# The last projection of a one-token attention kernel: wo in four loads, loop steps of eight, four column groups, one stored row

## The chip, the core and the metric

The kernel runs on one core of one Trainium2 chip. The time is the device's time of one execution in microseconds (us), of which medians are given. The profile shows one execution more closely. It calls TensorE "PE" (its weight loads "PEld"), VectorE "DVE", ScalarE "ACT", GpSimd "POOL", and SyncE's queue of DMA issues "SPq". The profile's "span" runs from its first to its last instruction; the time of the same run is 2.0 to 2.5 us longer. The granted clock is the share of TensorE's full clock that the throttle let through.

## The reference, cut to what matters

One token x of 512 elements. Branch A is attention of one query per head over 32 heads and 16384 stored keys and values of 128 elements each. Branch B is a small gated mixer. A gate g mixes the two.

```python
q = (x @ wq).reshape(1, 1, 32, 128)                      # 32 heads
p = softmax(q @ k_cache.T * 128 ** -0.5)                 # 16384 keys per head
a = (p @ v_cache).reshape(1, 1, 4096) @ wo               # wo: 4096 x 512
b = mixer(x, w_in, w_sp, b_sp, w_out)                    # 1 x 1 x 512
return g * a + (1 - g) * b                               # 1 x 1 x 512, bf16
```

Keys and values are 256 MB (2 x 32 x 16384 x 128 x 2 bytes). wo is 4 MB, the last that is loaded and the last that is used: out = sum over k of o2[:, k].T @ wo_k, for 32 slices wo_k of 128 x 512, with o2 the attention's result of 128 x 32.

## The kernel before

Keys and values stream through three buffers of 8 MB. wo goes into one of these buffers behind the last values, so its load starts when the last keys have been used. What matters here is the end: the loads of wo, the loop over k, and the store.

```python
WG = 4                                          # slices per loop step
WO_CUTS = (0, 8, 16, 24, 26, 28, 30, 31, 32)    # eight loads of wo, in slices of k
WIDE = 24                                       # slices done in the loop
# ... cut ...
def pe_wide(e):
    # ... cut: registers, waits for o2 ...
    with e.Fori(0, WIDE // WG) as t:            # six steps
        # ... four matmuls, k = 4t .. 4t+3, one in each column group of 32 of the array,
        #     each 1 x 512 into its own partition of the bank d_ps
        registers_first(nc, n, lambda: take(e, wo_s))    # wait for the load of these slices
        ins.then_inc(pe.sem, 1)
        warm(e, 1)                              # one matmul of 128x512 on zeros, to keep PE busy
        # ... registers ...
w_ok = act.op(lambda e: e.copy(out=d_sb[:, :], in_=d_ps), wait=[(pe.sem, pe.n)], mark=True)
for j, (a, b) in enumerate(zip(WO_CUTS[:-1], WO_CUTS[1:])):
    for k in range(max(a, WIDE), b):            # k = 24 .. 31
        for s in range(2):                      # two column groups of 256 columns
            # ... matmul into a_ps[32 * s], waits for load j before its first k
    if b == 28:
        # ... add: ones.T @ d_sb (fp32) into a_ps, in two halves of 256; waits for w_ok
r0_ok = dve.op(...copy a_ps[0, 0:256] to res[0, :]...)
r1_ok = act.op(...copy a_ps[32, 0:256] to res[32, :]...)
sp.op(lambda e: e.dma_start(out=out.rearrange("a b (c m) -> (a b c) m", c=2),
                            in_=res[0:33:32, :]), wait=[r0_ok, r1_ok], inc=(st_out, 16))
```

"k" below is such a slice of wo; one k is 1 KB in each of 128 partitions.

The softmax here doesn't subtract the row's maximum and nothing guards it: scores larger than these inputs give would overflow.

## Time and profile before

| | |
|---|---|
| time, median of the first 6 runs | 654.58 us (653.52 to 656.73) |
| profiled execution | 653.67 us, span 651.6 us |
| load queue | 279.58 MB, 99.4% of 16 engines' span |
| PE, DVE busy | 62%, 52% of the span |

The page of the kernel before, its parts 1 and 3 (busy us, share of the span, instructions; then queue, packets, MB, share of the 16 DMA engines):

```profile
span 651.6 us, 7678 instructions
...
PE 405.9 (62%) x2354; PEld 46.7 (7%) x1326; DVE 338.8 (52%) x162; ACT 43.5 (7%) x112; POOL 2.1 (0%) x9
...
q1 hardware_dynamic: 6772, 279.58, 99.4%
```

The loads fill the span. Only what follows the last byte can be anything else. The timeline of the last microseconds of the kernel before (start, duration, engine, line, operation, output <- inputs, count, and in brackets the idle time before it and what ended that):

```profile
643.55 0.39 PE L99 MATMUL ps_all<-bufs,o 128*1 x4 [0.48 <-PEq L82]
643.87 0.39 PE L443 MATMUL ps_all<-zero,ident 128*128 128x512 bf16 x1
644.31 0.39 PE L99 MATMUL ps_all<-bufs,o 128*1 x4
...
647.36 0.39 PE L99 MATMUL ps_all<-bufs,o 128*1 x4
...
648.00 0.60 PE L669 MATMUL ps_all<-bufs,o 128*1 128x256 bf16 x8
648.44 0.60 PE L676 MATMUL ps_all<-d_sb,const-float32-1.0 128*1 128x256 f32 x4
648.87 0.61 PE L669 MATMUL ps_all<-bufs,o 128*1 128x256 bf16 x8
...
649.51 0.41 DVE L680 CAST res<-ps_all 1x256 bf16<-1x256 f32 x1 [6.55 <-PE ps_all L669]
649.97 0.61 SPq L684 DMA_DIRECT2D out_dram<-res  x1
```

L99 is the loop (four matmuls a step, 0.75 us apart), L443 the warming matmul, L669 the last eight k, L676 the add. From 643.55 on the view marks idle time of PE before the first line alone: PE is working off a backlog. The view of the chain that ended last (start, duration, what) says the same. As far back as it goes, from 645.06 to the last matmul, it is PE's work, and no load is in it:

```profile
645.11 0.39 PE ps_all L99 x4
...
649.04 0.45 PE ps_all L669 x8
```

The loads of wo, in the view of their line:

```profile
L602 SPq DMA_DIRECT2D bufs<-in_A_wo_dram x8: 328/432/7735, 619.1 to 629.6; - x8
...
DMA to landing us min/median/max: 19.3/26.4/26.9
```

The last is issued at 629.6 and lands 19.3 us later, at 648.9. The last matmul ends 0.54 us after that (649.47 in the trace's records).

### The profile page before, as it was taken

What the parts mean: (1) busy time and instruction counts of PE and PEld (TensorE: products, weight loads), DVE (VectorE), ACT (ScalarE), POOL (GpSimd) and SP (SyncE); (2) the same over time, 40 slices, a digit from 0 to 9 for tenths busy, and PEclk for the clock granted to TensorE, in tenths of its full rate; (3) what the DMA queues carried; (4) which work ended last, traced back from release to release, by engine and by line L of the source; (5) the groups of instructions that cost most, each with busy time, mean ns of one, the idle gap of its engine ahead of it and who ended that gap; (6) DMA issues with size and microseconds to landing.
All of it is one profiled execution on the core that took longest, in us unless ns stands there. A gap on an engine that the chain in (4) does not pass through costs nothing. (4 is left out here: it accounts for less than half of the span.)

```text
span 651.6 us, 7678 instructions
## 1 busy us (share of the span) xinstructions
PE 405.9 (62%) x2354; PEld 46.7 (7%) x1326; DVE 338.8 (52%) x162; ACT 43.5 (7%) x112; POOL 2.1 (0%) x9
## 2 busy tenths in 40 slices
PE   4466856747386564747756375575737657477776
PEld 0100010000101000010000101000010100001012
DVE  4687708356280745618265470835629074565600
ACT  2101010000001000010100001000000100001011
POOL 1000000000000000000000000000000000000000
PEclk9678797969779696987969798786979968698979
DMA  9999999999999999999999999999999999999997
GB/s 388 439 437 451 435 426 426 451 435 402 451 451 426 410 451 439 435 414 451 435 426 426 451 435 406 447 451 426 410 451 439 435 414 451 435 416 437 426 419 314
DMA packets 6781, 279.60 MB, mean 429 GB/s; under 512 B 760, under 2 KB 1020, under 8 KB 1532
## 3 DMA queue, kind: packets, MB, share of 16 engines
q1 hardware_dynamic: 6772, 279.58, 99.4%
q8 instruction: 1, 0.02, 0.0%
q10 hardware_dynamic: 8, 0.00, 0.0%
HBM read 279.58 MB, written 0.00 MB: 429 GB/s over the span
## 5 line engine op out<-in xcount | busy, mean ns | idle before, releaser
L538 DVE TENSOR_TENSOR bufs<-bufs,qb x64 | 281.4, 4418 | 171.1 <-DVEq L82 171.1
L86 PE MATMUL ps_all<-bufs,ident 128*128 x960 | 261.9, 427 | 0.0
L456 PE MATMUL ps_all<-bufs,ident 128*128 x64 | 28.6, 447 | 157.0 <-PEq L82 157.0
L99 PE MATMUL ps_all<-bufs,p_t 128*8 x1024 | 79.8, 391 | 53.3 <-PEq L82 53.2
L522 DVE TENSOR_REDUCE s_sb<-ps_all 128x64 f32<-128x512 f32 x64 | 44.0, 688 | 95.5 <-DVEq L82 95.5
L550 ACT ACTIVATE p_t<-s_sb 64x256 f32 (+1 forms) x32 | 13.3, 414 | 440.4 <-ACTq L82 440.0
L456 PEld LDWEIGHTS ps_all<-bufs,ident 128*128 128x128 bf16 x64 | 6.3, 99 | 371.2 <-issue 371.2
L99 PEld LDWEIGHTS ps_all<-bufs,p_t 128*8 x1024 | 17.2, 82 | 164.4 <-issue 164.4
L490 PE MATMUL ps_all<-pick,d_sb 128*128 128x2 f32 x128 | 16.9, 254 | 14.8 <-PEq L82 14.8
L490 PEld LDWEIGHTS ps_all<-pick,d_sb 128*128 128x128 f32 x128 | 15.7, 192 | 26.3 <-issue 26.3
L559 ACT COPY d_sb<-ps_all 128x512 f32<-128x512 f32 x16 | 9.4, 585 | 104.5 <-ACTq L82 104.5
L443 PE MATMUL ps_all<-zero,ident 128*128 128x512 bf16 x25 | 9.7, 389 | 0.0
L86 PE MATMUL ps_all<-zero,ident 128*128 128x512 bf16 x32 | 9.5, 379 | 0.0
L564 ACT CAST ps_all<-zero 128x512 f32<-128x512 bf16 x15 | 8.8, 589 | 1.7
L360 PE MATMUL ps_all<-stats,const-float32-1.0 128*128 128x2 f32 x2 | 0.6, 362 | 9.2 <-DVE stats L358 9.2
L628 DVE RECIPROCAL rl<-ps_all 128x32 f32<-128x32 f32 x1 | 0.4, 358 | 11.3 <-PE ps_all L511 11.3
L631 DVE TENSOR_TENSOR o_sb<-ps_all,rl 128x32 bf16<-128x32 f32 x1 | 0.2, 192 | 11.5 <-PE ps_all L490 11.5
L550 ACT ACTIVATION_READ_ACCUMULATOR p_t<-s_sb (+1 forms) x32 | 5.9, 185 | 0.0
L99 PE MATMUL ps_all<-bufs,xb 128*64 x32 | 5.2, 498 | 0.1
L86 PE MATMUL ps_all<-bufs,xb 128*128 x12 | 4.8, 534 | 0.0
L337 DVE TENSOR_TENSOR bufs<-ps_all,ident 128x896 f32<-128x896 f32 x2 | 2.1, 1085 | 5.2 <-PE ps_all L86 5.2
L303 PE MATMUL ps_all<-xgw,const-float32-1.0 1*128 1x3 f32 x2 | 0.6, 360 | 6.4 <-DVE xgw L300 6.4
(73 smaller groups left out, 44.9 us busy)
## 6 DMA issues: line engine op xcount, KB each, us to landing
bufs<-in_A_k_cache_dram SPq DMA_DIRECT2D x4, 4096.0 KB, 33.5
bufs<-in_A_v_cache_dram SPq DMA_DIRECT2D x1, 5120.0 KB, 34.0
bufs<-in_A_wq_dram SPq DMA_DIRECT2D x1, 4096.0 KB, 17.8
bufs<-in_A_wo_dram SPq DMA_DIRECT2D x3, 1024.0 KB, 24.3
bufs<-in_A_v_cache_dram SPq DMA_DIRECT2D x1, 2048.0 KB, 38.6
bufs<-in_B_w_in_dram SPq DMA_DIRECT2D x1, 1792.0 KB, 7.4
bufs<-in_A_v_cache_dram SPq DMA_DIRECT2D x1, 1024.0 KB, 40.6
bufs<-in_B_w_out_dram SPq DMA_DIRECT2D x1, 896.0 KB, 8.5
```

What stands on the lines that cost most here:

```text
L86: ins = eng.matmul(out, lhsT=lhsT, rhs=rhs, **flags).ins
L99: ins = eng.matmul(bank[0:m, 0:n], lhsT=lhsT, rhs=rhs, **flags).ins
L303: g_ok = pe.op(lambda e: e.matmul(l_ps[:, 0:3], lhsT=ones_f[0:1, :], rhs=xgw[:, :], start=True, stop=True), wait=[xgw_ok], mark=True)
L337: dve.op(lambda e, h=h, zh=zh: e.tensor_tensor(out=zm[:, 2 * h * ZB:2 * (h + 1) * ZB].rearrange("p (b m k) -> p b m k", b=2, k=FhC), in0=z ...
L443: e.matmul(args[0], lhsT=args[1], rhs=args[2], **flags)
L456: matmul_on(nc, e, lambda: e.matmul(s3, lhsT=ident[:, :], rhs=k3[:, :, 0:W], start=True, **flags), [(kw, 0)])
L490: ins = e.matmul(o2, lhsT=d_sb[:, r * Dh:(r + 1) * Dh], rhs=pick[:, r * 2:(r + 1) * 2], start=False, stop=False, skip_group_check=True)
L522: return e.tensor_reduce(out=s_sb[:, c * QK:(c + 1) * QK], in_=s_ps[c % 2].rearrange("p (j w) -> p j w", w=W), axis=AX.X, op=ALU.add)
L538: e.tensor_tensor(out=k3, in0=k3, in1=qi, op=ALU.mult).then_inc(mul_s, 1)
L550: e.activation(out=p_t[rows, bass.ds(at, NG * 8)].rearrange("p (t c) -> p t c", c=8)[:, :, 4 * s:4 * s + 4], in_=s_sb[rows, :].rearrange(" ...
L559: return e.copy(out=d_sb[:, :], in_=d_ps)
L564: e.copy(out=d_ps, in_=zero[:, :]).then_inc(drn_s, 1)
```

## The change

Its intent: fewer and larger loads at the end; half as many loop steps, without warming matmuls; the last k in four column groups side by side; the result on one partition, stored as one row of 1 KB.

```diff
-WG = 4
+WG = 8
-WO_CUTS = (0, 8, 16, 24, 26, 28, 30, 31, 32)
+WO_CUTS = (0, 16, 24, 28, 32)
@@ pe_wide @@
-                    nc, e, d_ps, 32 * j, (1, D), o8[:, j:j + 1], w8[:, j * D:(j + 1) * D],
+                    nc, e, d_ps, 32 * (j % 4), (1, D), o8[:, j:j + 1], w8[:, j * D:(j + 1) * D],
-            warm(e, 1)
@@ last eight k, and the add of d_sb @@
-            for s in range(2):   # a_ps[32 * s, 0:256] += o2[:, k].T @ wo[k, s * 256:(s + 1) * 256]
+            for s in range(4):   # a_ps[32 * s, 0:128] += o2[:, k].T @ wo[k, s * 128:(s + 1) * 128]
@@ result @@
-    res = sb("res", [33, D // 2], BF16)
+    res = sb("res", [1, D], BF16)
-    (one copy of 256 by DVE to res[0], one of 256 by ACT to res[32])
+    (two copies of 128 by DVE, two by ACT, side by side in res[0])
-    sp.op(lambda e: e.dma_start(out=out.rearrange("a b (c m) -> (a b c) m", c=2),
-                                in_=res[0:33:32, :]), wait=[r0_ok, r1_ok], inc=(st_out, 16))
+    sp.op(lambda e: e.dma_start(out=out.rearrange("a b d -> (a b) d"), in_=res[:, :]),
+          inc=(st_out, 16))
```

The lines in parentheses and the two `for` lines stand for cut code. Cut altogether: setup edits (a memset moved from DVE to POOL, four copies of a selector made into one, the mixer's matmuls in four column groups with registers of their own).

More of the change, by code (lines that the diff above doesn't have):

```diff
@@ L18 @@
 DC = D // P
+DQ = D // 4
 HDh = H * Dh
@@ L185, in gated_mix_kernel @@
     eps_t = sb("eps_t", [P, 1], FP32)
-    sel = sb("sel", [H, 4 * P], BF16)
+    sel = sb("sel", [H, 4 * (P + 1)], BF16)
     pick = sb("pick", [P, 4 * 2], FP32)
@@ L254, in value @@
         return nc.snap(bass.RegisterHandles([reg]), min_val=0, max_val=top)
+    pool.op(lambda e: e.memset(eps_t[:, :], 1e-5), mark=True)
     pool.op(lambda e: e.memset(ident[:, :], 0.0), mark=True)
@@ L262, in gated_mix_kernel @@
     pool.op(lambda e: e.memset(zero[:, :], 0.0), inc=(exp_s, 1))
-    dve.op(lambda e: e.memset(eps_t[:, :], 1e-5), mark=True)
     const_ok = dve.op(lambda e: e.memset(sel[:, :], 0.0), mark=True)
@@ L287, in gated_mix_kernel @@
     xb_ok = dve.chain(lambda e: e.memset(m_ps[1], 0.0))
-    for i in range(4):
-        act.op(lambda e, i=i: e.copy(
-            out=sel[:, i * P:(i + 1) * P].rearrange("h (m i) -> h m i", i=4)[:, :, i],
-            in_=ident[0:H, 0:H]), wait=[const_ok, ident_ok] if i == 0 else (), mark=True)
+    act.op(lambda e: e.copy(
+        out=sel[:, :].rearrange("h (i x) -> h i x", x=P + 1)[:, :, 0:P:4],
+        in_=ident[0:H, 0:H].unsqueeze(1).broadcast_to([H, 4, H])), wait=[const_ok, ident_ok],
+        mark=True)
     dve.op(lambda e: e.tensor_reduce(
@@ L411, in pe_mixer @@
         e.wait_ge(ld_u, 16)
+        ua, wa = (counter(e, n, 0) for n in ("um", "wm"))
         with e.Fori(0, FhC) as k:
@@ L414, in pe_mixer @@
             wk = w_out[:, bass.ds(k * D, D)]
-            for s in range(2):
-                ins = matmul_at(nc, e, a_ps, 32 * s, (1, 256), uk, wk[:, s * 256:(s + 1) * 256],
-                                (u[:, 0:1], w_out[:, 0:256]))
+            n = len(nc.cur_bb.bb.instructions)
+            for s in range(4):
+                ins = matmul_on(nc, e, lambda: matmul_at(
+                    nc, e, a_ps, 32 * s, (1, DQ), uk, wk[:, s * DQ:(s + 1) * DQ],
+                    (u[:, 0:1], w_out[:, 0:DQ])),
+                    [(wa, in_setup + 2 * (DC * (HDh + F) + s * DQ)), (ua, 0)])
+            registers_first(nc, n)
             ins.then_inc(pe.sem, 1)
+            e.reg_alu(ua, ua, 2, ALU.add)
+            e.reg_alu(wa, wa, 2 * D, ALU.add)
     pe.raw(pe_mixer)
@@ L665, in gated_mix_kernel, with add @@
     w_ok = act.op(lambda e: e.copy(out=d_sb[:, :], in_=d_ps), wait=[(pe.sem, pe.n)], mark=True)
+    def add(lhsT, rhs, wait, mark=False):
+        for s in range(4):
+            ok = pe.op(lambda e, s=s: e.matmul(
+                a_ps[32 * s:32 * s + 1, 0:DQ], lhsT=lhsT, rhs=rhs[:, s * DQ:(s + 1) * DQ],
+                start=False, stop=False, skip_group_check=True), wait=wait if s == 0 else (),
+                mark=mark and s == 3)
+        return ok
     for j, (a, b) in enumerate(zip(WO_CUTS[:-1], WO_CUTS[1:])):
@@ L667, in gated_mix_kernel @@
         for k in range(max(a, WIDE), b):
-            for s in range(2):
-                y_ok = pe.op(lambda e, k=k, s=s: e.matmul(
-                    a_ps[32 * s:32 * s + 1, 0:256], lhsT=o2[:, k:k + 1],
-                    rhs=wo[:, k * D + s * 256:k * D + (s + 1) * 256], start=False, stop=False,
-                    skip_group_check=True), wait=[(ld_o[j], 16)] if k == a and s == 0 else (),
-                    mark=(k == H - 1 and s == 1))
-        if b == 28:
-            for s in range(2):
-                pe.op(lambda e, s=s: e.matmul(
-                    a_ps[32 * s:32 * s + 1, 0:256], lhsT=ones_f[:, 0:1],
-                    rhs=d_sb[:, s * 256:(s + 1) * 256], start=False, stop=False,
-                    skip_group_check=True), wait=[w_ok] if s == 0 else ())
@@ L680, in gated_mix_kernel @@
-    r0_ok = dve.op(lambda e: e.tensor_copy(out=res[0:1, :], in_=a_ps[0:1, 0:256]), wait=[y_ok],
-                   mark=True)
-    r1_ok = act.op(lambda e: e.copy(out=res[32:33, :], in_=a_ps[32:33, 0:256]), wait=[y_ok],
-                   mark=True)
-    sp.op(lambda e: e.dma_start(out=out.rearrange("a b (c m) -> (a b c) m", c=2),
-                                in_=res[0:33:32, :]), wait=[r0_ok, r1_ok], inc=(st_out, 16))
+            y_ok = add(o2[:, k:k + 1], wo[:, k * D:(k + 1) * D], [(ld_o[j], 16)] if k == a else (),
+                       k == H - 1)
@@ new lines, in gated_mix_kernel @@
+        if b == 28:
+            add(ones_f[:, 0:1], d_sb[:, :], [w_ok])
+    for q in (dve, act):
+        for s in (0, 1) if q is dve else (2, 3):
+            ok = q.op(lambda e, s=s, copy=(q is act): (e.copy if copy else e.tensor_copy)(
+                out=res[0:1, s * DQ:(s + 1) * DQ], in_=a_ps[32 * s:32 * s + 1, 0:DQ]),
+                wait=[y_ok] if s % 2 == 0 else (), mark=True)
+        sp.raw(lambda e, ok=ok: e.wait_ge(*ok))
+    sp.op(lambda e: e.dma_start(out=out.rearrange("a b d -> (a b) d"), in_=res[:, :]),
+          inc=(st_out, 16))
```

## The prediction

> **What bounds it now.** The loads. The page's DMA queue part puts the one load queue at 279.58 MB and 99.4% of all 16 engines' span, 429 GB/s. [...] PE (62% of the span) and DVE (52%) have slack. So only two things can move the time: how soon the last byte lands, and the tail behind it.
>
> **The tail now** (timeline of the last 10 us, span 651.6). The last load of wo, 1 KB per partition, is issued at 629.6 and lands 19.3 us later, at 648.9 (the wo loads' line). The windows view agrees: DMA share 1.05 in 646-647, 0.77 in 647-648, 0.17 in 648-649. PE is late by itself: six loop steps, four matmuls and one warming matmul each, repeat every 0.75 us from 643.55 to 648.0; then eight 256-column matmuls (648.00), the add of the copied bank (648.44, waiting for a 0.58 us ACT copy), and eight more (648.87 to 649.48). DVE and ACT copy 256 elements each side by side (0.41 and 0.36 us, from 649.51), the store is issued at 649.97 and the span ends at 651.6, 1.6 us later.
>
> **What the change does.**
> 1. wo in four loads: 16, 8, 4, 4 KB per partition for 8, 8, 8, 2, 2, 2, 1, 1. Packets in the trace take 0.046 us at 1 KB, 0.085 at 2 KB, 0.313 at 8 KB, 0.615 at 16 KB. My estimate for 4 KB, between these, is 0.16. The last MB lands in about 2.58 us instead of 2.67, the first 3 MB 0.05 sooner: last landing about 0.15 us earlier, 648.8.
> 2. Three steps of eight without warming: as in the value loop, 0.60 us busy, 0.9 us apart. The first two can start only when the 2 MB load lands (643.7), the third when k 16-24 lands (646.2), so the loop ends near 647.0, not 648.0. That makes PE wait for the loads again, which earns nothing more than the landing allows.
> 3. The last four k: 16 matmuls of 128 columns in four groups. Before, a pair of 256 columns started every 0.108 us; four at a time should start every 0.055. From last landing to last matmul about 0.45 us (now 0.55).
> 4. Four copies of 128, two per engine: I estimate 0.48 us per engine instead of 0.41, as fixed cost is paid twice. Loss 0.06. [...] One descriptor of 1 KB instead of two of 512 B: no more than 0.05 gained of the 1.6 us.
> 5. Setup (one selector copy for four, memset moved, mixer with four groups): off the critical path, since loads are already queued to beyond 50 us.
>
> **Critical part.** 0.15 + 0.1 + 0.03 - 0.09: about 0.2 us of 654.6.
>
> **Prediction.** 654.4 us, range 653.3 to 655.4 (single executions of before spread over 3.2 us, more than the effect). Faster by over 2%: 0.01; within 2%: 0.98; slower: 0.01.
>
> **Signs.** Load queue still above 99%; last wo landing at 648.7-648.9; PE idle between the loop steps; last matmuls 0.4-0.5 us after the landing; copies over 0.45-0.5 us; span 651.3-651.6.
>
> **What could be wrong.** Without warming, PE's clock may be halved at the end. [...] this trace shows granted clock 0.50 at 622-625 and 632-635, after windows under half busy. It would add about 0.2 us to the last matmuls, cancelling the gain. Or the landing may depend on the slowest engine and not on packet size; or four-group matmuls may be bound by issue, not columns.

Cut from this text, where marked, are two statements that no trace shows and the term of 0.03 us for one more semaphore wait, whose source is not given and which no trace shows. The forecast's sum was 0.15 + 0.1 + 0.03 - 0.09 = 0.19, "about 0.2 us": landing, PE's lateness, and store, less 0.09 for the copies, of which 0.06 still stands in the text and 0.03 was the cut wait.

## The result, and the profile after

| | before | after |
|---|---|---|
| time, median | 654.58 us (653.52 to 656.73, 20 runs) | 653.95 us (653.59 to 654.24, 10 runs) |
| profiled execution | 653.67 us, span 651.6 | 653.97 us, span 651.4 |
| load queue | 99.4% | 99.4% |

The ratio is 0.9989, 95% interval 0.998 to 0.9998. The profiled time of after, 653.97 us, is at its median. The medians differ by 0.63 us. More striking is the spread: 3.2 us before, 0.65 us after; 11 of the 20 runs of before are slower than the slowest of after.

The page of the kernel after, the lines that answer to those above:

```profile
span 651.4 us, 7703 instructions
...
PE 404.5 (62%) x2382; PEld 45.8 (7%) x1354; DVE 339.1 (52%) x162; ACT 43.5 (7%) x110; POOL 2.1 (0%) x10
...
q1 hardware_dynamic: 6194, 279.58, 99.4%
```

The timeline of the kernel after:

```profile
644.02 1.93 PE L100 MATMUL ps_all<-bufs,o 128*1 x16 [0.82 <-PEq L83]
...
646.51 1.02 PE L100 MATMUL ps_all<-bufs,o 128*1 x8 [0.56 <-PEq L83]
...
647.65 0.59 PE L676 MATMUL ps_all<-bufs,o 128*1 128x128 bf16 x16
...
648.96 0.59 PE L676 MATMUL ps_all<-bufs,o 128*1 128x128 bf16 x16
...
649.61 0.59 DVE L690 CAST res<-ps_all 1x128 bf16<-1x128 f32 x2 [6.49 <-PE ps_all L676]
650.24 0.32 SPq L694 DMA_DIRECT2D out_dram<-res  x1
```

And the loads of wo, in the view of their line:

```profile
L610 SPq DMA_DIRECT2D bufs<-in_A_wo_dram x4: 328/432/435, 619.8 to 621.1; - x4
...
  PEld ps_all L676: 1.7, 2
...
DMA to landing us min/median/max: 24.0/26.6/27.8
```

PE now waits for loads: the last two loads have a weight load of L676 waiting for them (PE's weight loads were idle for 1.7 us before these two). The chain that ended last now comes out of the last load:

```profile
621.12 27.80 DMA bufs<-in_A_wo_dram
...
648.96 0.63 PE ps_all L676 x14
```

The last load lands at 621.1 + 27.8 = 648.9, as before. The copies take longer (0.59 us on DVE instead of 0.41), the store's issue is shorter (0.32 us instead of 0.61) and the end follows 1.16 us after it instead of 1.61.

These two profiles together explain 0.2 us of span and say nothing about the spread. They also differ in something else. The granted clock in windows around the end (columns: window, its length, PE busy and count, granted clock, DMA share, GB/s), first of the kernel before:

```profile
644.00:646.00 2.00, 1.82 (x15) 1.00 0.98 388
646.00:648.00 2.00, 1.91 (x15) 1.00 0.91 323
```

then of the kernel after:

```profile
644.00:646.00 2.00, 1.93 (x16) 0.50 1.00 408
646.00:648.00 2.00, 1.37 (x24) 0.50 0.74 297
```

The kernel after was profiled with PE at half clock in its last 8 us, the kernel before at full clock. The comparison is of a lucky execution of one with an unlucky one of the other.

### The profile page after: what moved, and what is told of

The parts are those of the page before. It is cut to its first block, busy times and chain, and to the rows that moved or that the text cites. A ratio compares the mean times of both kernels' runs of the same rounds, so it can differ in the third digit from the quotient of the medians.

```text
span 651.4 us, 7703 instructions
## 1 busy us (share of the span) xinstructions
PE 404.5 (62%) x2382; PEld 45.8 (7%) x1354; DVE 339.1 (52%) x162; ACT 43.5 (7%) x110; POOL 2.1 (0%) x10
## 3 DMA queue, kind: packets, MB, share of 16 engines
q1 hardware_dynamic: 6194, 279.58, 99.4%
## 5 line engine op out<-in xcount | busy, mean ns | idle before, releaser
L87 PE MATMUL ps_all<-bufs,ident 128*128 x960 | 262.8, 429 | 0.0
L87 PE MATMUL ps_all<-zero,ident 128*128 128x512 bf16 x32 | 9.5, 379 | 0.0
L451 PE MATMUL ps_all<-zero,ident 128*128 128x512 bf16 x19 | 7.4, 389 | 0.0
L87 PE MATMUL ps_all<-bufs,xb 128*128 x12 | 4.0, 454 | 0.0
```

Source lines behind the costliest of these rows:

```text
L87: ins = eng.matmul(out, lhsT=lhsT, rhs=rhs, **flags).ins
L451: e.matmul(args[0], lhsT=args[1], rhs=args[2], **flags)
```

## The experiments

Theory A: in the kernel before, PE works off a backlog at the end, so the time depends on whether its clock is halved just then; after the change PE has time to spare and hardly depends on it. Rivals: B, the loads' landing makes the difference; C, the store does. Twelve runs were made. Every result was correct. "Time less span" is the mean over a kernel's runs.

| kernel | median us (range) | ratio to before (95%) | spans us | time less span |
|---|---|---|---|---|
| before, again | 654.43 (653.89 to 655.42) | 0.999 (0.9974 to 1.0005) | 651.9 to 653.4 | 2.00 |
| before + loop of eight | 653.86 (653.50 to 654.51) | 0.9986 (0.9969 to 1.0002) | 651.4 to 652.5 | 2.01 |
| before + four loads | 655.08 (654.70 to 656.35) | 1.0003 (0.9986 to 1.002) | 652.7 to 654.4 | 1.96 |
| before + one row | 654.28 (653.52 to 656.05) | 0.999 (0.9971 to 1.0009) | 651.3 to 653.9 | 2.20 |
| after, two rows | 654.07 (653.99 to 654.52) | 0.9997 (0.9981 to 1.0012) | 651.7 to 652.2 | 2.32 |
| before, no warming | 654.62 (654.33 to 656.27) | 1.001 (0.9992 to 1.0028) | 652.3 to 654.3 | 2.00 |
| after, two pieces on one partition | 654.12 (one run) | none | 651.8 | 2.3 |
| after + warming | 653.86 (653.54 to 654.80) | 0.9994 (0.9978 to 1.001) | 651.1 to 652.3 | 2.48 |
| after, again | 653.80 (653.46 to 654.02) | 0.9989 (0.9972 to 1.0006) | 651.0 to 651.5 | 2.47 |
| before + loop + one row | 653.97 (653.19 to 654.34) | 0.9991 (0.9974 to 1.0008) | 651.0 to 652.2 | 2.16 |
| after with two column groups | 653.91 (653.20 to 654.20) | 0.9988 (0.997 to 1.0005) | 651.0 to 652.1 | 2.15 |
| the mix | 653.80 (653.18 to 653.98) | 0.9988 (0.9971 to 1.0005) | 651.1 to 651.9 | 2.11 |

The runs of before that stood beside these had medians of 654.49 (first four), 653.86 (next four) and 654.30 us (last four), so a median of before by itself is uncertain by some 0.3 us. The kernel before against itself (first row) is at 0.999, as far from 1 as most of the others. The causes are read from the traces: the time of the last landing (the last increment that the last load of wo makes to its semaphore), of the last matmul's end, of the store, and the stretches at half clock, from the trace's own records. All in us from the span's start; differences in the text are those of the rounded times here:

| profiled execution | clock at half | last landing | last matmul ends | store issued | span ends |
|---|---|---|---|---|---|
| before, as first profiled | not in the end | 648.93 | 649.47 | 649.97 | 651.58 |
| before, again | 641.60 to 648.43 | 649.21 | 651.33 | 651.82 | 653.43 |
| before + loop of eight | not in the end | 648.99 | 649.31 | 649.80 | 651.42 |
| before + four loads | 643.62 to 650.45 | 648.77 | 651.85 | 652.34 | 653.95 |
| before + one row | 644.15 to 647.56 | 649.18 | 650.50 | 650.99 | 652.15 |
| before, no warming | 646.33 to 649.74 | 648.98 | 650.23 | 650.73 | 652.34 |
| after, as first profiled | 643.28 on | 648.92 | 649.55 | 650.24 | 651.40 |
| after, again | 641.60 to 648.42 | 649.02 | 649.46 | 650.14 | 651.30 |
| after, two rows | 641.75 on | 648.79 | 649.43 | 650.11 | 651.72 |
| after with two column groups | 644.44 on | 648.95 | 650.36 | 650.85 | 652.01 |
| before + loop + one row | 646.50 to 649.91 | 649.28 | 650.15 | 650.64 | 651.80 |
| after, two pieces on one partition | 641.54 to 648.36 | 648.94 | 649.38 | 650.06 | 651.79 |
| after + warming | 650.12 on | 649.04 | 649.48 | 650.16 | 651.32 |
| the mix | 644.07 to 647.48 | 648.94 | 649.96 | 650.45 | 651.61 |

### The kernel before, again

No edit.

> The kernel before, unchanged, to see where its spread comes from (653.5 to 656.7 us, while the kernel after stays within 653.6 to 654.2). Theory A (the tail of the kernel before is PE's own, so its time depends on whether PE's clock is halved there): spans of these runs again spread over 2 us or more, and a slow one shows the six loop steps 0.85 us apart instead of 0.75 and the last matmuls at about twice the spacing, with the last load landing at the same 648.9. Theory B (the loads are late in the slow runs): the last landing itself moves with the span.

Its profile fell in a slower execution, and that is the one to look at. Its timeline:

```profile
644.39 0.60 PE L99 MATMUL ps_all<-bufs,o 128*1 x4 [0.27 <-PEq L82]
...
644.92 0.61 PE L443 MATMUL ps_all<-zero,ident 128*128 128x512 bf16 x1
...
645.46 0.60 PE L99 MATMUL ps_all<-bufs,o 128*1 x4
...
649.85 0.60 PE L669 MATMUL ps_all<-bufs,o 128*1 128x256 bf16 x8
...
650.72 0.61 PE L669 MATMUL ps_all<-bufs,o 128*1 128x256 bf16 x8
```

and its granted clock by window:

```profile
644.00:646.00 2.00, 1.73 (x11) 0.50 0.97 383
646.00:648.00 2.00, 2.00 (x14) 0.50 0.91 322
```

At half clock the steps are 1.07 us apart instead of 0.75 (the expectation said 0.85: too little). The last landing is 0.28 us later than in the first profile, but the last matmul is 1.86 us later and the span 1.85 us longer. So the backlog of PE makes 1.58 us of the difference (2.12 us from landing to the last matmul instead of 0.54), the landing 0.28. In the clock records of the first profiles of before and after, the stretches at half clock that end within the span last 3.41 us or a multiple of it, up to 13.65. They begin at different places of the same program (641.60 here; in the first profile of the same kernel the last one of the span ended at 635.23). What makes the clock fall is not shown. Only two executions of before were profiled, so that this explains the whole spread is in part argued. But each run has its mean granted clock beside its span. In 37 runs of before (spans 651.5 to 654.4) the two go together (correlation -0.63, where 0 is none and -1 is perfect): the seven runs at a clock of 0.846 have spans of 651.7 to 652.5, the 13 at 0.830 or below 652.2 to 654.4. In 17 runs of after they do not (0.14): the eight at 0.830 or below have spans of 651.0 to 651.8. The clock here is that of the whole execution and not of its end, so the tie can't be tight.

### The loop of eight alone

```diff
-WG = 4
+WG = 8
-                    nc, e, d_ps, 32 * j, ...
+                    nc, e, d_ps, 32 * (j % 4), ...
-            warm(e, 1)
```

> The kernel before with the loop part alone: three steps of eight, no warming matmul; still eight loads, two column groups, two rows stored. Theory A (PE was late in the tail): most of the gain of the whole change in the median, ratio about 0.9990 to before, and a spread under 1.2 us; loop over before 647.0 at full clock. Theory B (the loads decide): ratio 1.000 and the spread of before. Theory C (the store gives the gain): ratio 1.000, the stretch from store issue to the end still 1.6 us.

The median is 653.86 us, 0.6 under before's of the same rounds, and the spans lie within 1.1 us. Its timeline:

```profile
644.54 0.60 PE L99 MATMUL ps_all<-bufs,o 128*1 x8 [0.31 <-PEq L82]
646.37 0.60 PE L99 MATMUL ps_all<-bufs,o 128*1 x8 [1.22 <-PEq L82]
...
649.03 0.27 PE L668 MATMUL ps_all<-bufs,o 128*1 128x256 bf16 x2 [0.20 <-DMA bufs<-in_A_wo_dram]
```

PE now idles before its third step (1.22 us) and before the last k, which it starts 0.04 us after the landing. The last matmul ends 0.32 us after the landing. That is theory A as expected; the interval of the ratio just reaches 1, so the size rests on the trace. This profile is at full clock. At half clock the loop of eight is late too (0.87 us from landing to the last matmul, in "loop and store together" below).

### Four loads alone

```diff
-WO_CUTS = (0, 8, 16, 24, 26, 28, 30, 31, 32)
+WO_CUTS = (0, 16, 24, 28, 32)
```

> The kernel before with wo in four loads alone; loop of six steps with warming, two column groups, two rows. Theory A: no gain, ratio 1.000 within 0.0005, spread still above 1.5 us, as PE is late anyway. Theory B (packet size and landing decide): last landing 0.1 to 0.2 us after-to-before sooner, ratio 0.9990 and a narrow spread. Theory C: ratio 1.000.

This part alone is no gain; in its profile the loads land sooner (648.77) and the work ends later:

```profile
643.95 0.60 PE L99 MATMUL ps_all<-bufs,o 128*1 x4 [0.81 <-PEq L82]
...
651.25 0.60 PE L669 MATMUL ps_all<-bufs,o 128*1 128x256 bf16 x8
```

The first step has to wait for a load of 2 MB instead of 1 MB (which landed at 643.77; it starts at 643.95 instead of 643.55), and then come the same six steps, here at half clock: the last matmul ends 3.08 us after the landing. Its quickest span of six, 652.7, is 1.2 us above the quickest of before. As the gain of the whole change, theory B falls. The larger packets do what was estimated: a packet of 4 KB takes 0.16 us. From the landing of the last values to that of the last wo, 9.89 to 10.03 us pass in the seven profiles with these four loads, and 10.11 to 10.27 in the six with eight. But the landing itself moved by as much from run to run (648.77 to 649.28 in the table).

### The store alone

```diff
-    res = sb("res", [33, D // 2], BF16)
+    res = sb("res", [1, D], BF16)
-    (copies to res[0, :] and res[32, :]; two rows stored)
+    (copies to res[0, 0:256] and res[0, 256:512]; one row stored)
```

> The kernel before with the store alone changed: both 256-element copies go to one partition and one row of 1 KB is stored. Theory C (the store gives the gain: in the profile after, issue to end took 1.14 us against 1.59): the store's issue takes 0.32 us instead of 0.61, end 0.40 to 0.45 us sooner in every run, ratio 0.9993; the spread stays. Theories A and B: the issue stays at 0.6 us and the ratio at 1.000.

The store's issue in its timeline:

```profile
650.99 0.32 SPq L684 DMA_DIRECT2D out_dram<-res  x1
```

0.32 us instead of 0.61, and 1.16 us from issue to the span's end instead of 1.61. Nothing else on the path changed, so theory C is right about 0.45 us of the span, in addition to A. The time shows less: time less span is 2.20 us in these runs and 2.00 without the edit. So about 0.25 us of the 0.45 are left in the time. What ends an execution after the span is not in the profile; that POOL's clearing of semaphores, which ends 0.28 us before the span's end with two rows and 0.12 with one, sets the pace there is a guess that fits. It fits more than these two: from the end of that clearing to the end of the time (with anything that lies before the span's start) 2.27 to 2.37 us pass in all nine profiles of kernels built from before, whether two rows are stored or one. On that reading the time gains what the issue gains, 0.29 us. The spread stayed (spans 651.3 to 653.9), as A says.

### The kernel after with two rows stored

```diff
-    res = sb("res", [1, D], BF16)
+    res = sb("res", [33, D // 2], BF16)
-    (four copies side by side in res[0]; one row stored)
+    (four copies, two in res[0] and two in res[32]; two rows stored)
```

> The kernel after, with only the store undone: the four copies go to two partitions and two rows of 512 B are stored. The run with the one-row store alone took the stretch from store issue to the end from 1.61 us to 1.16, by a shorter issue. If that is a property of the store, this run shows 0.61 us for the issue and 1.6 us to the end, spans 0.45 us above those of the kernel after (651.4 becomes 651.85, time about 654.4), with the narrow spread kept. If the gain of the whole change is all PE's, spans stay at 651.4.

```profile
650.11 0.61 SPq L694 DMA_DIRECT2D out_dram<-res  x1
```

The issue is back at 0.61 us and the end at 1.61 us after it; spans are 651.7 to 652.2 against 651.1 to 651.8, and the spread stays narrow. That settles the store's part of the span from the other side. In the time, two rows cost 0.12 us of the median (654.07 and 653.95, from different rounds).

### Two pieces on one partition

```diff
-    in_=res[:, :]                      # [1, 512]
+    in_=(two pieces of 256 with a gap of 32 elements, both in partition 0)
```

> The kernel after with the result still on one partition, but stored as two pieces of 512 B with a gap between them. If two partitions made the old store's issue long, the issue stays at 0.32 us; if the number of pieces [...] did, it takes 0.6 us and the end comes 1.6 us after the issue.

```profile
650.06 0.74 SPq L694 DMA_DIRECT2D out_dram<-res  x1
```

0.74 us, and 1.73 us to the end: the number of pieces makes the issue long, not the two partitions. In the first profile of before the store's instruction carries two elements of 512 B and two packets of 512 B move, 0.025 us each; in that of after it carries one element of 1 KB and one packet moves, 0.045 us. The packets differ by far less than the issue, and why the issue is longer with two pieces is not shown.

### The kernel before without warming matmuls

```diff
             ins.then_inc(pe.sem, 1)
-            warm(e, 1)
```

> The kernel before with only the warming matmul of the loop taken away; still six steps of four, eight loads. Theory A1 (the warming matmuls were PE's delay): steps repeat in about 0.55 us at full clock and 0.65 at half, the loop is held by the loads and ends before 647.0, median about 653.9 as with three steps of eight. Theory A2 (the fixed cost of a step was the delay, so that eight per step was needed): steps stay at 0.7 us or more and the median stays near 654.5. If warming held the clock up, the trace shows more half-clock stretches after 643 than before.

```profile
643.60 0.39 PE L99 MATMUL ps_all<-bufs,o 128*1 x4 [0.48 <-PEq L82]
644.36 0.39 PE L99 MATMUL ps_all<-bufs,o 128*1 x4 [0.38 <-PEq L82]
...
647.41 0.59 PE L99 MATMUL ps_all<-bufs,o 128*1 x4 [0.15 <-PEq L82]
```

The steps are still 0.75 us apart, with PE idle 0.36 to 0.41 us before each after the first at full clock: there the warming matmul filled a gap and cost nothing. What sets the step is the work of PE's sequencer between two steps (the timeline puts that idle time down to it, PEq L82; the trace has three register operations, a branch and the wait for the load there, one after the other, from 644.41 to 645.10 between the second step and the third). At half clock it does cost: the last step here starts 0.75 us after the one before it although the clock is at half, where the kernel before needs 1.07. So of the two parts of the loop edit, eight matmuls a step are what shortens the loop (0.91 us for eight instead of 1.5), and leaving the warming out protects it when the clock is low. The median, 654.62 us, shows no gain; the runs of before beside it had a quick spell (653.86), so this run settles the step's length, not the time.

### The kernel after with warming matmuls

```diff
         with e.Fori(0, WIDE // WG) as t:
+            warm(e, 2)
```

> The kernel after with two warming matmuls at the top of each of the three steps, where PE waits for loads anyhow. The profile of the kernel after had the clock at half from 643.3 on, and its last 16 matmuls took 0.63 us from landing to end. If PE's clock is what is left to gain, this run has full clock from about 647 on, the last matmuls take 0.42 us, and spans fall by up to 0.2 us (651.4 to 651.2). Rival: warming delays the steps (0.85 us per pair at half clock) and spans rise or stay.

In the first profiles of before and after, matmuls of the line that multiplies by ident (L86, L87) mostly start 0.427 us apart at half clock, two of which are 0.85, and 0.216 us apart at full.

```profile
649.08 0.39 PE L677 MATMUL ps_all<-bufs,o 128*1 128x128 bf16 x16 [0.67 <-DMA bufs<-in_A_wo_dram]
```

The clock was full to 650.1 in this execution and the last matmuls took 0.44 us from landing to end, against 0.63 in the first profile of after. But the kernel after, again, shows the same 0.44 us without warming: its clock had come back at 648.42. So 0.19 us is what a low clock costs the kernel after, and whether the warming secured it is not shown: one of five spans was 652.3, longer than any of after. No gain.

### The kernel after, again, and three combinations

The kernel after ran once more on the chip of the last three.

> The kernel after, unchanged, on the same chip as the three below. Spans 651.1 to 651.8 as on record (median time 653.95), in narrow spread whatever PE's clock is at the end.

As expected: spans 651.0 to 651.5.

Loop and store together, without the rest:

```diff
-WG = 4
+WG = 8
-            warm(e, 1)
-    res = sb("res", [33, D // 2], BF16)
+    res = sb("res", [1, D], BF16)
 (with 32 * (j % 4), two copies of 256 into res[0], one row stored)
```

> The kernel before with the loop part and the one-row store together; still eight loads, two column groups, two copies of 256. If the two parts are independent: the spans of the loop part alone (651.4 to 652.5) less 0.45 us, so 650.95 to 652.05, median time about 653.5, ratio about 0.998 to before. At full clock its profile should end near 651.0, below the kernel after; at half clock near 652, above it. Rival: what the loop gives and what the store gives are the same gain, and the median stays at 653.9.

The range of spans, 651.0 to 652.2, is close to that expected for independent parts (650.95 to 652.05), but most runs lay in its upper half, and the mean span is 0.17 us under that of the loop alone (651.78 and 651.95), not 0.45. The median was expected at 653.5 and came out at 653.97, which is what the rival said. With six runs each, over different rounds, that decides nothing; that the two gains add up is shown by the trace alone, where the end follows the store's issue by 1.16 us as with the one row. Its profile, at half clock from 646.50, needs 0.87 us from landing to the last matmul.

Two column groups in place of four (which also leaves the setup as it was before):

```diff
 (the edits of the combination above, and)
-WO_CUTS = (0, 8, 16, 24, 26, 28, 30, 31, 32)
+WO_CUTS = (0, 16, 24, 28, 32)
```

> The kernel after with four column groups of 128 and four copies undone: two groups of 256, two copies; four loads, three steps of eight and the one-row store stay (the setup edits are undone too, they are off the critical path). Copies take 0.41 us instead of 0.59. At full clock from landing to last matmul 0.65 us (0.44 with four groups), so equal to the kernel after within 0.1 us; at half clock about 1.1 us against 0.63, so spans up to 0.3 us longer. Median time 653.9 to 654.3 and a wider spread than after. If four groups bring nothing, it is 0.2 us faster than after in every run.

```profile
649.30 1.06 PE L668 MATMUL ps_all<-bufs,o 128*1 128x256 bf16 x8
650.40 0.41 DVE L679 CAST res<-ps_all 1x256 bf16<-1x256 f32 x1 [7.30 <-PE ps_all L668]
```

At half clock 1.41 us pass from landing to the last matmul (expected 1.1), because PE is late again: it was still at the add of d_sb at the landing (648.95) and came to the last k at 649.30. With four groups it was 0.63 us at half clock. The copies take 0.41 us and not 0.59. So, with these two parts read from the traces, four groups gain where the clock is low and lose about 0.2 us in the copies always. The spans say the same: 651.0 to 652.1 here, 651.0 to 651.5 for after in the same rounds; the medians differ by 0.1 us. The setup edits differ as well, so the narrower spread is not shown to come from the groups alone. Against "loop and store together" this run has only the four loads more: mean spans of 651.63 and 651.78 us, too close to tell whether the loads gain their 0.15 us once PE is on time.

The mix, meant to beat both:

```diff
 (the edits of "loop and store together", and)
-WO_CUTS = (0, 8, 16, 24, 26, 28, 30, 31, 32)
+WO_CUTS = (0, 16, 24, 28, 30, 32)
         with e.Fori(0, WIDE // WG) as t:
+            warm(e, 2)
```

> A version meant to beat both: the kernel before with the loop part, the one-row store, wo in five loads (16, 8, 4, 2, 2 KB per partition, so only two k are left after the last landing), two groups of 256, and two warming matmuls at the top of each of the three steps. At full clock: landing 649.0, last matmul 0.42 us later, copies 0.41, store 1.2: span about 651.1 or less, median time 653.5. If the clock halves all the same, 651.6.

```profile
643.95 0.95 PE L99 MATMUL ps_all<-bufs,o 128*1 x8
...
645.80 1.02 PE L99 MATMUL ps_all<-bufs,o 128*1 x8
...
647.63 0.60 PE L99 MATMUL ps_all<-bufs,o 128*1 x8
```

It ties with the kernel after (653.80 us both) and does not beat it. In its profile the clock fell to half in the first step (644.07 to 647.48), and with two warming matmuls a step the second began 1.85 us and the third 3.68 us after the first; PE was late once more, with the last matmul 1.02 us after the landing. In this execution, warming a clock that was already low, ahead of work that was due, cost what it was to save.

## Why the prediction was right, and where it was not

The time, 653.95 us, lies in the range, and "within 2%" was right. The gain was expected at 0.2 us and is 0.63 by medians. That the time fell into the range says little: the range was 2.1 us wide, more than any error below. And that the span of the two first profiles fell by 0.18 us, close to the 0.2 of the sum, is luck: its terms are far from those that were predicted (last paragraph but one). Point by point:

- What bounds the kernel: right. The load queue stays at 99.4% and the bytes are the same.
- "PE is late by itself": right, and the heart of the matter, but mis-sized. The sum gave it 0.1 us, read from one execution at full clock. In another execution of the same kernel the same backlog ended 2.12 us after the landing instead of 0.54. The median of before contains such executions; the profile that the prediction was read from does not. The spread of 3.2 us was on the table and was taken for noise; it was the thing that the change removes.
- The loop: right in length ("0.9 us apart", the end near 647.0; 0.91 us, and 646.96 at full clock in the profile of the loop of eight alone). That it "earns nothing more than the landing allows" was not right: even at full clock the loop alone brought the last matmul from 0.54 to 0.32 us after the landing, and at half clock the gain is larger. Which of the two edits shortens the loop was not asked; it is the eight per step, and the warming cost nothing at full clock.
- The loads: the estimate of 0.16 us for a packet of 4 KB and of 0.15 us for the whole is about right (10.13 to 9.97 us from the last values to the last wo, 10.17 to 9.96 in the mean of all profiles with eight loads and with four), but the landing did not come earlier in the first profile of after (648.92 after 648.93), since in that execution the last of a load's 16 increments was 0.11 to 0.15 us later from the first load of keys on (29.09 after 28.98, and 638.95 after 638.80 for the last values). The lag is there from the start and stays: from the first increment to the last, that first load took 1.06 us and the last load of values 1.10 in the first profile of before, 1.22 and 1.30 in that of after. The four loads alone gained nothing.
- The last four k: "about 0.45 us" is 0.44 at full clock and 0.63 at half.
- The copies: estimated at 0.48 us, measured 0.59. The second copy on DVE starts 0.31 us after the first, with none of the overlap that the estimate gave it; one copy of 128 took 0.28 us there, where one of 256 took 0.41. The second wait does not show: from the last copy's end to the store's issue 0.04 us pass in both.
- The store: "no more than 0.05" was wrong by a factor of nine in the span: 0.45 us, and about 0.25 of it in the time. The prediction counted descriptors and had no term for the issue.
- The fear of a halved clock: it came true in the first profile of after and cost 0.19 us there, but the kernel before suffers more from it, with warming matmuls and all (half clock from 641.60 in its second profile). Leaving them out was not what let the clock fall: it fell at 643.28, before the loop began. That idle time lowers the clock, as the fear had it, is not shown. The half clock that the prediction names (621.58 to 624.99 and 631.82 to 635.23) did come after 3.41 us in which PE was busy for 1.46 and 1.36 us. But at 643.28 it came after 3.03 us of 3.41 busy, at 641.60 in the second profile of before after 2.15 of 3.40, and in the first profile of before the clock stayed full through 635.23 to 638.64 and after it, with PE busy for 1.88 of 3.41. So PE's busy time just before does not by itself tell when the clock falls. Whether leaving them out keeps it low is open: of the profiles with half clock before the last matmul, it stayed low to the span's end in three of seven without warming in the loop, and in none of four with it.

Sum for the span from the second profile of before to the first of after: landing 0.29 sooner, landing to last matmul 1.49 shorter, copies and waits 0.20 longer (0.69 us after 0.49), store 0.45 shorter; together 2.03, which is 653.43 less 651.40. From the first profile of before: 0.01, minus 0.09, minus 0.19 and 0.45, together 0.18. The fairest pair is the second profile of before and that of "after, again", as both had half clock from 641.60 to 648.43 (648.42): landing 0.19 sooner, landing to last matmul 1.68 shorter (2.12 and 0.44), copies and waits 0.19 longer, store 0.45 shorter, together 2.13.

One thing is left open. On average the span became 1.14 us shorter (652.57 over 31 runs of before, 651.43 over 11 of after), the time only 0.66 (means of the same runs; the 11 are of other rounds than the 31. In the rounds of "after, again", with both side by side, it is 1.25 and 0.80). The other half went outside the span: time less span is 2.02 us for before and 2.50 for after. About 0.2 of it comes with the one-row store (2.00 to 2.20). The other 0.3 comes with what after and its variants have and the combinations built from before lack, the setup edits or the four column groups with their four copies: 2.32 against 1.96 to 2.02 with two rows stored, 2.47 to 2.50 against 2.11 to 2.20 with one. Counted from POOL's clearing it is the same step: 2.61 to 2.72 us in the five profiles of after and its variants, 2.27 to 2.37 in the nine others. No run tells the two causes apart, and the profile does not show what happens there.

## What to carry to other kernels

If executions of one kernel spread more than the gain that is sought, find out first what a fast and a slow one differ in; here the tail of PE's work met a clock at half rate or not, and a single profile showed only the kind case. Work behind the last byte should be so short that the slowest clock still keeps up with the loads: fewer loop steps and shorter matmuls bought evenness (times within 0.65 us instead of 3.2) more than speed (0.63 us of the median). Small things at the very end count: one stored row instead of two was worth 0.45 us of the span (about 0.25 of the time), where the loop of eight brought 0.22 at full clock.
